# A recurrence followed by an FFN on one core: six more steps whose instructions keep the source's order

## The chip, the cores and the metric

The kernel runs on one core of a Trainium2 chip. The metric is the device time of one execution in microseconds; three executions of the kernel before gave 325.9, 326.82 and 327.14, the median is 326.82. The core has four engines that compute, each with its own queue of instructions, which it works off strictly in order: TensorE (PE; weight loads are listed apart as PEld), VectorE (DVE), ScalarE (ACT) and GpSimd (POOL). SyncE (SP) issues the transfers.

## What is computed

A chunked linear recurrence over 4 x 8 heads of 768 tokens (head size 32, state size 16), and then a feed-forward layer with softplus over all 3072 tokens (256 to 2048 to 256). Cut to what matters:

```python
for c in range(nc):                          # chunks of 32 tokens
    cum = np.cumsum(log_a[chunk])
    M = (C @ B.T) * causal * exp(cum_i - cum_j)
    y = M @ x + (C @ state) * exp(cum)
    state = exp(sum(log_a)) * state + (B * exp(cum_last - cum)).T @ x
h = y_of_all_heads @ w_in                    # 3072 x 256 @ 256 x 2048
g = softplus(h)
out = g @ w_out                              # 3072 x 2048 @ 2048 x 256
```

## The kernel before

**Tiles and units.** The recurrence is worked in 24 units of 128 tokens (unit i = 6 b + u for batch b). The FFN is worked in six tiles of 512 tokens, j = 0 to 5; tile j needs units 4 j to 4 j + 3. For each tile there are 16 slices k of 128 hidden columns.

**The FFN's steps.** A step s stands for one (j, k). Its order over s is: tile 0, k 0 to 7; tile 1, k 0 to 7; tile 0, k 8 to 15; tile 1, k 8 to 15; and from s = 32 on tile 2 and so on, 16 steps each. In step s TensorE does the second product `acc` (six matmuls, in the two `acc` banks) for step s - 4 and the first product `hp` (six matmuls) for step s. The tiles between the two products are `e` (ACT, softplus of hp, L720), `gh` (ACT, its high part, L726) and `gl` (DVE, its low part, L732). Where a tile begins in the `acc` banks (s = 36 for tile 2) `hp` goes ahead of `acc`. When tile 1 is done, in step 35, `finish_part` (L800) adds the half that was kept before: two DVE instructions `o<-acc,half` (L803), one for each `acc` bank, followed by their stores. There is one buffer for each `acc` bank, so the next tile's first product into a bank waits for its `o`.

**The recurrence's work beside it.** From unit 12 on it is spread over the steps, with s0 = 30 + 4 (i - 12):
- step s0 - 4 (28 for unit 12): `split_whole(i)`. ACT then DVE make `c_all` (for even units in `kc`; for odd ones in the tag `c_all` with one buffer) and `b_rows` (two buffers) from the loaded `bc` (ACT L290, DVE L292); between them SP stores `c_all` into `c_rows`, which exists once.
- step s0: `attend_scores(i)`. POOL makes `rm` (L402, two buffers); TensorE `sp` twice, each followed on DVE by `m<-sp,rm` (L457); then DVE `bp` (L417, not for the last unit of a batch) and `cc` (L433, not for the first).
- step s0 + 1: `prefetch(i + 3)`: SP loads `un`, then `bc`, and for even units `gg`.
- for odd i, steps s0 + 2 and s0 + 3: `pair_values` and `pair_ends` of units i - 1 and i (TensorE `zp`, `yp`; DVE `state`, `tb`, `y`, `xl`; ACT `xh`).

So step 31 loads unit 15; step 34 holds `attend_scores(13)` and then `split_whole(14)`; step 35 the two `o` of tile 1 and the loads of unit 16; step 36 `pair_values(12)`; step 37 `pair_ends(12)`; step 38 `attend_scores(14)` and then `split_whole(15)`.

**What sets the order.** The framework has a planner that puts each engine's instructions in an order of its own, by when it reckons their inputs to be there. TensorE's instructions and SP's transfers are always kept in the source's order. For DVE, ACT and POOL, `InOrder` (L118 to L131) does so only while `in_order[0]` is true: each such instruction is pinned behind the instruction that the source issued before it on its engine. An instruction that isn't pinned may be put ahead of pinned ones. Everything up to step 30 is pinned: first what the list `ORDER` gives, which covers the first 28 steps' `hp` and 24 steps' `acc`, then a loop that starts at `AHEAD` = 28 and ends the pinning at `PINNED`:

```python
    for s in range(AHEAD, len(steps) + LAG):
        if s == PINNED:
            in_order[0] = False
        if begins(*steps[s - LAG]):
            begin(s)
        values(s)
        begin(s)
        for f, args in fills[s]:
            f(*args)
```

`in_order[0]` has a second use, in `load_unit` (L252): while it is true and i is 12 or more, a one-element DVE memset of the new `bc` tile stands ahead of its load.

```python
            if in_order[0] and i >= FIRST:
                V.memset(both[:1, :1, :1], 0)
```

All pinned instructions of DVE, ACT and POOL, and all of TensorE's, show the line of the wrapper, L129, in the profile; all transfers show L139.

Of the kernel before, what the change touches and what calls it, by code (L numbers as in the profile page):

```python
# [75 lines left out]
"""  # L76
HALF = NFT // 2
AHEAD = 28
PINNED = 31
LAG = 4  # L80
WRAW = 4
EARLY = 8
# [24 lines left out]
def recurrence_then_ffn(ctx: ExitStack, tc: tile.TileContext, fst, un, alr, w_in, w_out, const, outT):  # L107
# [826 lines left out]
# [3 lines that stand above are left out]
# [63 lines left out]
```

## Time and profile before

| what | us |
|---|---|
| time, median of 3 (lowest to highest) | 326.82 (325.9 to 327.14) |
| the profiled execution's own time | 326.83 |
| its span | 325.1 |
| TensorE busy | 318.3 |
| DVE busy | 190.6 |
| ACT busy | 191.1 |
| POOL busy | 39.4 |

Times in the profile are microseconds from the start of the span. In a timeline row stand the start, the length, the engine (SPq is SyncE's queue), the line, the operation, the tile written and those read, the shape, the number of instructions, and in square brackets the engine's idle time before it with what ended it. In a row of the waits: who waited for whom, us in total, how often, and the longest. A row of stretches has its bounds, its length, the busy time of PE, PEld, DVE, ACT and POOL with the instructions in brackets, the granted TensorE clock, the share of the DMA engines and GB/s. On TensorE a matmul is followed by the next one after some 0.23 us, though its own row is longer, because they are pipelined.

### The profile page before, as it was taken

The page shows a single profiled execution, that of the slowest core. Times are in us where ns is not written, and L with a number is a line of the kernel's source. Part 1 is how long each engine was busy: PE and PEld are TensorE (multiplying, and loading weights), DVE is VectorE, ACT ScalarE, POOL GpSimd, SP SyncE. Part 2 cuts the span into 40 slices and gives each one's busy share as a digit, 9 for nine tenths or more (in the row PEclk, how much of TensorE's full clock was granted, in tenths as well). Part 3 has the DMA queues.
Part 4 walks back from the last instruction along what each step waited for, and adds up shares of the span by engine and source line. Part 5 has one row for each costly group of instructions (what it writes and reads, how often), then busy time and mean ns, then how long its engine had stood idle before and what let it go on. Part 6 is the DMA issues. An engine that isn't in the chain of part 4 may idle for free.

```text
span 325.1 us, 5266 instructions
## 1 busy us (share of the span) xinstructions
PE 318.3 (98%) x1974; PEld 255.7 (79%) x1974; DVE 190.6 (59%) x338; ACT 191.1 (59%) x349; POOL 39.4 (12%) x42
## 2 busy tenths in 40 slices
PE   8999999999999999899999999999999999999996
PEld 3568888888878888588888888888888888888885
DVE  3799767889584566775646746675744433322222
ACT  4898989797877565544433824644633344544450
POOL 3545300210300001102202101012100000000000
PEclk9999999999999999999999999999999999999999
DMA  6949658661732154335125246125201000100001
GB/s 222 394 152 359 212 187 214 176 194 46 246 100 66 65 151 124 107 124 143 32 99 159 70 130 146 51 97 161 86 14 34 0 2 0 53 12 2 1 0 65
DMA packets 25178, 36.53 MB, mean 112 GB/s; under 512 B 2112, under 2 KB 13504, under 8 KB 25152
## 3 DMA queue, kind: packets, MB, share of 16 engines
q1 hardware_dynamic: 25152, 36.19, 36.0%
q8 instruction: 15, 0.25, 0.3%
q14 instruction: 11, 0.09, 0.1%
HBM read 28.74 MB, written 3.24 MB: 98 GB/s over the span
## 4 chain that ended last, share of the span: by engine, by line
PE 88%; DVE 4%; DMA 3%; SPq 2%; issue 2%; ACT 0%; POOL 0%; DVEq 0%; ACTq 0%; POOLq 0%
PE hp L129 38%; PE acc L129 37%; PE yp L129 6%; PE sp L129 4%; PE warm L129 2%; DMA un<-in_un 2%; SPq L139 2%; DMA bc<-in_un 1%; PE zp L129 1%; PE end L129 1%; DVE m L129 1%; DVE w L129 1%; PE gp L129 0%; DVE b_rows L292 0%; DVE o L803 0%
## 5 line engine op out<-in xcount | busy, mean ns | idle before, releaser
L732 DVE TENSOR_TENSOR gl<-e,gh 128x512 fp32r<-128x512 f32 x65 | 49.8, 771 | 50.0 <-ACT gh L726 48.9
L129 PE MATMUL hp<-xh,wih 128*128 128x512 f32 (+1 forms) x204 | 77.6, 380 | 0.0
L129 PE MATMUL hp<-xl,wih 128*128 128x512 f32 (+1 forms) x204 | 76.9, 377 | 0.0
L129 PE MATMUL hp<-xh,wil 128*128 128x512 f32 (+1 forms) x204 | 76.8, 377 | 0.0
L720 ACT ACTIVATE e<-hp 128x512 f32<-128x512 f32 x65 | 38.7, 595 | 64.6 <-PE hp L129 64.2
L129 PE MATMUL acc<-gh,woh 128*128 128x512 f32 x188 | 74.9, 399 | 1.5 <-DVE o L803 1.5
L129 PE MATMUL acc<-gh,wol 128*128 128x512 f32 x188 | 73.4, 390 | 0.1
L129 PE MATMUL acc<-gl,woh 128*128 128x512 f32 x188 | 73.5, 391 | 0.0
L129 PEld LDWEIGHTS hp<-xh,wih 128*128 128x128 f32 x204 | 38.4, 188 | 8.3 <-DVE xl L129 1.0
L726 ACT CAST gh<-e 128x512 fp32r<-128x512 f32 x65 | 40.2, 619 | 6.7 <-PE acc L129 4.0
L129 PEld LDWEIGHTS hp<-xh,wil 128*128 128x128 f32 x204 | 38.3, 188 | 7.1
L129 PEld LDWEIGHTS hp<-xl,wih 128*128 128x128 f32 x204 | 38.4, 188 | 6.9
L129 PEld LDWEIGHTS acc<-gh,woh 128*128 128x128 f32 x188 | 35.4, 188 | 9.0 <-DVE o L803 1.4
L129 PEld LDWEIGHTS acc<-gh,wol 128*128 128x128 f32 x188 | 35.3, 188 | 8.1 <-DVE wol L129 0.6
L129 PEld LDWEIGHTS acc<-gl,woh 128*128 128x128 f32 x188 | 35.4, 188 | 6.4 <-DVE gl L732 0.2
L402 POOL TENSOR_SCALAR_AFFINE_SELECT rm<-fc 128x1024 f32<-128x1024 f32 x11 | 16.8, 1531 | 129.8 <-DVE m L457 97.2
L129 DVE TENSOR_TENSOR gl<-e,gh 128x512 fp32r<-128x512 f32 x31 | 21.5, 701 | 9.6 <-ACT gh L129 9.5
L129 POOL TENSOR_SCALAR_AFFINE_SELECT rm<-fc 128x1024 f32<-128x1024 f32 x13 | 19.0, 1466 | 63.5 <-DVE m L129 58.4
L129 ACT ACTIVATE signs<-wraw 128x512 f16<-128x512 f32 (+1 forms) x32 | 24.1, 776 | 0.0
L129 ACT ACTIVATE e<-hp 128x512 f32<-128x512 f32 x31 | 18.2, 594 | 7.5 <-PE hp L129 7.2
L129 ACT CAST gh<-e 128x512 fp32r<-128x512 f32 x31 | 19.0, 617 | 3.5 <-PE acc L129 3.3
L129 DVE TENSOR_TENSOR m<-sp,rm 128x512 f32<-128x512 f32 x26 | 17.2, 681 | 1.0 <-PE sp L129 1.0
(103 smaller groups left out, 306.8 us busy)
## 6 DMA issues: line engine op xcount, KB each, us to landing
bc<-in_un SPq DMA_DIRECT2D x16, 512.0 KB
wraw<-in_w_in SPq DMA_DIRECT2D x8, 512.0 KB
wraw<-in_w_out SPq DMA_DIRECT2D x8, 512.0 KB
un<-in_un SPq DMA_DIRECT2D x16, 256.0 KB
out_t<-o SPq DMA_DIRECT2D x9, 256.0 KB
gg<-gd SPq DMA_DIRECT2D x16, 128.0 KB
c_rows<-c_all SPq DMA_DIRECT2D x16, 128.0 KB
c_rows<-kc SPq DMA_DIRECT2D x16, 128.0 KB
```

Of the source, the lines that this page charges most:

```text
L129: return lambda *a, **k: tc.keep_in_program_order(f(*a, **k))
L139: tc.keep_in_program_order(nc.sync.dma_start(out, in_))
L402: Pl.affine_select(out=rm.rearrange("p h c i -> p (h c) i"), in_=fc[:, u].rearrange("p h c -> p (h c)").unsqueeze(2).broadcast_to([P, NH * ...
L720: A.activation(e, h, AF.Softplus)
L726: A.copy(gh, e)
L732: V.tensor_tensor(gl, e, gh.bitcast(F32), op=ALU.subtract)
```

## The change

`PINNED` goes from 31 to 37, nothing else:

```diff
-PINNED = 31
+PINNED = 37
```

With it `in_order[0]` stays true for steps 31 to 36. On ACT and DVE the `e`, `gh` and `gl` of these steps, `attend_scores(13)`, `split_whole(14)`, the two `o` of tile 1 and the DVE part of `pair_values(12)` are now pinned in this order. The loads of units 15 and 16 (steps 31 and 35) each get the memset ahead of their `bc`. What comes from step 37 on is free as before.

## The prediction

> **What bounds the kernel now.** I read the page first, then the table of stretches, the waits of TensorE, and the order of instructions of each engine around the places where TensorE stands still. Unit 13, step 34 and so on are counted off in source order, because the profile leaves buffer numbers out. L129 marks an instruction issued while the order is kept; the same instruction issued later shows its own line (L290, L433, L720).
>
> ```profile
> span 325.1 us, 5266 instructions
> PE 318.3 (98%) x1974; PEld 255.7 (79%) x1974; DVE 190.6 (59%) x338; ACT 191.1 (59%) x349; POOL 39.4 (12%) x42
> 88.00:92.50 4.50, 4.27 (x57) 3.09 (x57) 3.51 (x8) 3.04 (x6) 1.06 (x1) 1.00 0.35 81
> 92.50:134.30 41.80, 41.80 (x188) 34.27 (x186) 25.34 (x44) 26.68 (x47) 1.41 (x1) 1.00 0.33 99
> 134.30:138.00 3.70, 2.23 (x27) 1.25 (x30) 3.67 (x5) 1.28 (x4) 1.28 (x1) 1.00 0.29 108
> 138.00:285.00 147.00, 147.00 (x919) 121.67 (x908) 80.23 (x132) 70.74 (x120) 12.87 (x8) 1.00 0.28 79
> PE acc L129 <- DVE o L803: 1.5, 2, 0.9
> ```
>
> In a row of stretches the first number after the bounds is the length, the next the busy time of PE. TensorE is busy 318.3 of 325.1 us, and between 92.5 and 285 us it stands still in one stretch only, 134.3 to 138.0, for 3.70 - 2.23 = 1.47 us. Its order is the source's in both kernels, its granted clock is 1.00 in these rows. So the change can gain only what lies in this gap and in the 0.23 us of the first stretch, and it loses whatever new idle time it puts on TensorE. This is the gap, and the orders of DVE, ACT and POOL that make it:
>
> ```profile
> 134.97 0.47 PE L129 MATMUL acc<-gh,woh 128*128 128x512 f32 x1 [0.55 <-DVE o L803]
> ...
> 136.82 0.50 PE L129 MATMUL acc<-gh,woh 128*128 128x512 f32 x1 [0.92 <-DVE o L803]
> ...
> 137.72 0.43 PE L129 MATMUL zp<-un,bp 128*32 128x64 f32 x16
> ```
>
> ```profile
> 132.28 0.75 DVE L292 SCALAR_TENSOR_TENSOR c_all<-bc,kb,c_all 128x512 fp32r<-128x512 f32 x1 [1.86 <-ACT c_all L290]
> 132.94 1.28 DVE L457 TENSOR_TENSOR m<-sp,rm 128x512 f32<-128x512 f32 x2
> 134.14 0.68 DVE L803 TENSOR_TENSOR o<-acc,half 128x512 f32<-128x512 f32 x1
> 134.74 1.43 DVE L292 SCALAR_TENSOR_TENSOR b_rows<-bc,kb,b_rows 128x512 fp32r<-128x512 f32 x1
> 136.09 0.68 DVE L803 TENSOR_TENSOR o<-acc,half 128x512 f32<-128x512 f32 x1
> 136.69 1.28 DVE L732 TENSOR_TENSOR gl<-e,gh 128x512 fp32r<-128x512 f32 x2
> ```
>
> ```profile
> 127.15 0.60 ACT L720 ACTIVATE e<-hp 128x512 f32<-128x512 f32 x1 [1.47 <-PE hp L129]
> 127.78 0.62 ACT L726 CAST gh<-e 128x512 fp32r<-128x512 f32 x1
> 131.52 0.72 ACT L290 ACTIVATE c_all<-bc,kb 128x512 fp32r<-128x512 f32 x1 [3.11 <-DMA bc<-in_un]
> 132.15 0.58 ACT L720 ACTIVATE e<-hp 128x512 f32<-128x512 f32 x1
> 132.63 0.71 ACT L290 ACTIVATE b_rows<-bc,kb 128x512 fp32r<-128x512 f32 x1
> 133.24 0.61 ACT L726 CAST gh<-e 128x512 fp32r<-128x512 f32 x1
> ```
>
> ```profile
> 134.36 1.28 POOL L402 TENSOR_SCALAR_AFFINE_SELECT rm<-fc 128x1024 f32<-128x1024 f32 x1 [11.29 <-DVE m L457]
> ```
>
> The second product of tile 2 begins in banks that the two o instructions of tile 1 (step 35) must first read. The first o ends at 134.82, the second at 136.77, and TensorE follows at 134.97 and 136.82. They are late because c_all of unit 15, which the source has in step 38, was put ahead of e of step 34 on ACT and ahead of m of unit 13 on DVE, and its data came 3.11 us after ACT had reached it. On the other hand the planner had put gl of step 34 (136.69), bp, cc and both splits of unit 14 out of the way of o.
>
> **The change part by part.** Steps 31 to 36 keep the source's order on DVE, ACT and POOL. Instructions of step 37 and later stay free. I take it, from the code and from the tiles standing in source order in every group that I looked at, that the buffers of one tag are given out in source order. Then bp and cc of units 14 and 15 and b_rows of unit 15 can't pass unit 13's and 14's. But c_all of unit 15 has a tag of its own that only odd units use, so it can still go ahead.
>
> *Removed: cc of unit 13 from 88.71.* It waited for its unit's load with everything behind it:
>
> ```profile
> 88.71 0.48 DVE L433 TENSOR_TENSOR cc<-un,fr 128x128 f32<-128x128 f32 x1 [1.10 <-DMA un<-in_un]
> 89.11 0.68 DVE L129 SCALAR_TENSOR_TENSOR w<-w,signs 128x512 int32<-128x512 int32 x1
> ...
> 89.73 0.06 DVE L129 MEMSET bc<- 1x1 int32 x1
> ```
>
> ```profile
> 89.91 0.40 PE L129 MATMUL acc<-gl,woh 128*128 128x512 f32 x1
> 90.46 0.50 PE L129 MATMUL acc<-gh,wol 128*128 128x512 f32 x1
> ```
>
> ```profile
> 91.25 0.39 PE L129 MATMUL acc<-gh,wol 128*128 128x512 f32 x1
> 91.71 0.71 PE L129 MATMUL yp<-cc,tb 128*128 128x128 f32 x4
> ```
>
> ```profile
> 87.78 1.28 POOL L402 TENSOR_SCALAR_AFFINE_SELECT rm<-fc 128x1024 f32<-128x1024 f32 x1
> ```
>
> At the pitch of 0.23 us between products, 90.46 - 89.91 - 0.23 = 0.32 is lost at the first pair and 91.71 - 91.25 - 0.23 = 0.23 at the second, 0.55 in all. But the next instruction on DVE, w, would now stand beside rm of unit 13, which runs to 87.78 + 1.28 = 89.06, as POOL's order doesn't change. Such pairs block each other: b_rows at 134.74, beside rm at 134.36, takes 1.43 instead of 0.75 and ends at 136.17, 0.53 after rm's end at 135.64. So w ends at about 89.06 + 0.53 = 89.59 instead of 89.79: a gain of **0.2 us**, bounds 0 and 0.55 (no blocking).
>
> *Added: two one-element memsets* (units 15 and 16), each ahead of its bc load, behind gl of steps 31 and 35. A memset of this kind takes 0.06 us (the row at 89.73). Unit 15's buffer was last read by unit 12's split, long done, so the memset waits for nothing, and SP reaches that bc load only at 127.22, after the two c_rows stores and un below, while gl of step 31 is done by about 125. Cost 0; bounds 0 and 0.06 each on DVE.
>
> *Moved on DVE ahead of m of unit 13 and of o:* gl of step 34, then behind m: bp and cc of unit 13, kc and b_rows of unit 14, then the two o. I work it out by assuming that c_all of unit 15 keeps its place ahead of e on ACT, because what makes it free there does not change much: TensorE's order, bc's place in SP's queue. When does its data come?
>
> ```profile
> 123.12 0.74 DVE L129 SCALAR_TENSOR_TENSOR c_all<-bc,kb,c_all 128x512 fp32r<-128x512 f32 x1
> ```
>
> ```profile
> 121.65 1.41 POOL L402 TENSOR_SCALAR_AFFINE_SELECT rm<-fc 128x1024 f32<-128x1024 f32 x1 [32.59 <-DVE m L129]
> ```
>
> ```profile
> 123.92 2.62 SPq L139 DMA_DIRECT2D c_rows<-c_all  x2
> ...
> 127.22 0.45 SPq L139 DMA_DIRECT2D bc<-in_un  x1
> 130.34 1.29 SPq L139 DMA_DIRECT2D c_rows<-kc  x2
> ```
>
> The bc load stands behind the c_rows stores, and those behind c_all of unit 13, which ends at 123.86. Without the two bp ahead of it c_all of unit 13 would start near 121.65, but beside rm, so it ends at 121.65 + 1.41 + 0.53 = 123.6: 0.25 earlier, and ACT's c_all starts at 131.27. (The two stores take 2.62 us here and 1.29 at 130.34; if this falls away too, it is 1.3 us earlier yet. I keep that for the range.) From 131.27, with the pitches of the rows above:
> - ACT: c_all 131.27, e + 0.63 = 131.90, gh + 0.63 = 132.53, done 133.15.
> - DVE: gl of step 34 at 133.18, m at + 0.61 = 133.79, both done at + 1.28 = 135.07.
> - POOL's rm of unit 15 starts 0.14 after m (134.22 to 134.36), so 135.21; bp gets in before it, cc waits: rm from about 135.25 to 136.55.
> - kc at 136.60 (c_all at 123.12 stood 0.06 behind the end of rm), b_rows + 0.66 = 137.26, o + 0.66 = 137.92, second o + 0.60 = 138.52.
> - TensorE: first product at o + 0.83 = 138.75 (134.14 to 134.97), second + 0.77 = 139.52, zp + 0.75 = 140.27, against 137.72.
>
> That is **+2.55 us** in the place of the 1.47 us wait, so that the gap there becomes about 4 us. Bounds of this term: +1.2 (the stores at 1.29) and +2.8 (bc not earlier at all). [...]
>
> *Moved elsewhere:* bp and cc of unit 14 and cc of unit 15 leave their early places; they come after step 36, where DVE has 147.00 - 80.23 = 66.8 us free. c_rows of unit 14 are stored near 137.3 instead of 130.34 and are read by TensorE in step 38, past 144, so that is hidden too; if that cover went, TensorE would wait for the store's landing there. gh of step 36 waits for the product's end as before, and state and tb behind it are due only at yp of step 37, some 3 us later.
>
> Sum: 2.55 - 0.2 = +2.35 on the profiled execution's 326.83 us (span 325.1 and 1.73 around it; the median is 326.82, the same): **329.2 us**.
>
> **The rivals.**
> 1. *c_all of unit 15 doesn't go ahead of gh any more* (its memset, or the shorter queue in front, puts its load past gh in the planner's reckoning). Then e starts when its hp ends, a step's 12 products of 0.227 behind the e at 127.15: 129.87, gh 130.50, gl 131.15, m 131.76 to 133.04, rm to 134.50, kc 134.55, o 135.87, TensorE 136.70, zp 138.22: +0.5 - 0.2, **327.1 us**. Without the blocking by rm o starts 1.15 earlier and zp comes at 137.1: 326.0. For it: ACT's place for c_all lies within one wait for hp (128.4 to 129.85). Against: nothing ahead of its load grows by more than 0.06 us. This ends on the other side, not slower; the point from which it decides is whether bc counts as landed before hp of step 34.
> 2. *c_all goes between e and gh:* gh starts 0.63 earlier than in the forecast, **328.6 us**.
> 3. *DVE's row goes on and rm waits for it* (cc, kc and b_rows follow bp without a break, rm runs beside o): o starts near 136.8, 1.15 less than the forecast, **328.0 us**. For it: DVE has an instruction ready at every end. Against: at 121.65 rm went ahead of the bp that was next on DVE.
> 4. *The change does nothing here:* the planner's order of DVE comes out with the same wait at o: **326.8 us**. Against: gl, bp, cc, kc and b_rows stand ahead of o in the source, and the chain is kept.
>
> **How the numbers follow.** Forecast 0.55, rival 1 0.22, rival 2 0.08, rival 3 0.10, rival 4 0.05. The forecast's own bounds are 1.2 - 0.2 and 2.8, so 327.8 to 329.6. Within 0.5% means 325.2 to 328.5, about what a measurement of this kernel can tell from no change. Of the forecast some 0.45 lies above that and 0.10 within (short stores); rival 2 is half and half; rivals 1, 3 and 4 lie within, but for 0.04 that I keep for gains that no row shows, on top of rival 1 unblocked and the whole 0.55 (325.7). Slower 0.50, same 0.46, faster 0.04. The range runs from rival 1 (327.1, less some of its unblocked form) to the forecast's upper bound with 0.2 us for an unseen stall: 326.5 to 329.8.
>
> **What would show it.** Right: no DVE row of cc near 88.7 waiting for un; on ACT c_all waiting about 3 us for bc near 128 to 131, ahead of e; on DVE gl, m twice, bp, cc, kc, b_rows, o, o in one row between 133 and 139; a wait of acc for o of 3 to 4.5 us and nowhere else one over 0.3. Wrong: e of step 34 right behind hp (rival 1), rm behind b_rows (rival 3), a new wait of TensorE at sp of step 38 for c_rows or at hp of step 37 (bp and cc made late matter after all), or o ahead of kc.

## The result and the profile after

| | median, us | lowest to highest | ratio to the kernel before |
|---|---|---|---|
| before | 326.40 (4 runs) | 325.9 to 327.14 | 1 |
| changed | 330.76 (4 runs) | 329.77 to 332.17 | 1.0135, interval 1.009 to 1.018 |

The change makes the kernel slower by 4.4 us. The forecast had 329.2 us, slower by 2.35, in a range that ended at 329.8: the sign was right, the size was half of it. The profiled execution of the changed kernel took 329.77 us, the fastest of its four.

The head of the changed kernel's page:

```profile
span 328.0 us, 5267 instructions
PE 318.7 (97%) x1974; PEld 256.7 (78%) x1974; DVE 191.4 (58%) x340; ACT 190.9 (58%) x349; POOL 39.9 (12%) x42
```

Its waits of TensorE (us in total, times, longest):

```profile
PE acc L129 <- DVE o L129: 4.2, 1, 4.2
```

Its stretches (bounds, length, busy time of PE, PEld, DVE, ACT and POOL, granted clock, DMA share, GB/s):

```profile
84.00:92.50 8.50, 8.44 (x75) 6.46 (x74) 7.92 (x15) 6.84 (x13) 2.95 (x2) 1.00 0.64 209
134.30:145.00 10.70, 7.50 (x69) 5.81 (x70) 7.37 (x17) 1.23 (x3) 0.60 (x1) 0.84 0.46 147
145.00:285.00 140.00, 140.00 (x849) 115.86 (x848) 76.45 (x124) 68.02 (x116) 12.86 (x8) 1.00 0.27 72
```

One wait of TensorE stands where two stood before: 4.2 us for the first o, in the place of 1.5 for both. From 145 to 285 us TensorE is busy without a break, as before. But the granted clock of the stretch from 134.30 to 145 is 0.84, where the kernel before had 1.00 in all its rows from 88 to 285 us. The same stretch of the changed kernel, cut at 138.06, where the products' rows grow longer, and at 141.48, with as much ahead of it and behind it:

```profile
134.65:138.06 3.41, 0.56 (x3) 0.50 (x4) 3.41 (x8) 0.26 (x1) 0.25 (x1) 1.00 0.16 36
138.06:141.48 3.42, 3.42 (x45) 2.48 (x47) 2.27 (x6) 0.62 (x1) 0.00 (x0) 0.50 0.61 194
141.48:144.90 3.42, 3.42 (x30) 2.72 (x23) 1.34 (x5) 0.00 (x0) 0.00 (x0) 1.00 0.67 230
```

TensorE's timeline there:

```profile
132.90 0.39 PE L129 MATMUL hp<-xh,wil 128*128 128x512 f32 x1
137.50 0.47 PE L129 MATMUL acc<-gh,woh 128*128 128x512 f32 x1 [4.21 <-DVE o L129]
...
138.43 0.63 PE L129 MATMUL acc<-gh,woh 128*128 128x512 f32 x1
138.86 0.63 PE L129 MATMUL acc<-gl,woh 128*128 128x512 f32 x1
139.28 0.63 PE L129 MATMUL acc<-gh,wol 128*128 128x512 f32 x1
139.85 0.65 PE L129 MATMUL zp<-un,bp 128*32 128x64 f32 x16
140.28 1.64 PE L129 MATMUL yp<-m,un 128*32 128x128 f32 x32
141.84 0.50 PE L129 MATMUL acc<-gh,woh 128*128 128x512 f32 x1
142.18 0.39 PE L129 MATMUL acc<-gl,woh 128*128 128x512 f32 x1
```

What to see here: from 138.06 to 141.48 the clock is half. The products stand 0.43 us apart instead of 0.23, and yp takes 1.64 instead of 1.06. From 142.18 on a product's row is 0.39 long again instead of 0.63. So the wait is followed by a second loss that is no wait and shows in no list of waits.

Why o is late is to be read from the timelines of the changed kernel, first ACT's:

```profile
126.03 0.60 ACT L129 ACTIVATE e<-hp 128x512 f32<-128x512 f32 x1 [1.47 <-PE hp L129]
129.05 0.72 ACT L290 ACTIVATE c_all<-bc,kb 128x512 fp32r<-128x512 f32 x1 [2.42 <-DMA bc<-in_un]
129.68 0.60 ACT L129 CAST gh<-e 128x512 fp32r<-128x512 f32 x1
130.19 0.59 ACT L129 ACTIVATE e<-hp 128x512 f32<-128x512 f32 x1
130.81 0.62 ACT L129 CAST gh<-e 128x512 fp32r<-128x512 f32 x1
```

Then DVE's:

```profile
131.47 0.69 DVE L129 TENSOR_TENSOR gl<-e,gh 128x512 fp32r<-128x512 f32 x1 [0.31 <-ACT gh L129]
132.08 1.28 DVE L129 TENSOR_TENSOR m<-sp,rm 128x512 f32<-128x512 f32 x2
133.28 0.28 DVE L129 TENSOR_TENSOR bp<-un,ft 128x128 f32<-128x128 f32 x1
133.47 0.28 DVE L129 TENSOR_TENSOR cc<-un,fr 128x128 f32<-128x128 f32 x1
133.68 1.35 DVE L417 TENSOR_TENSOR bp<-un,ft 128x128 f32<-128x128 f32 x1
134.95 0.48 DVE L433 TENSOR_TENSOR cc<-un,fr 128x128 f32<-128x128 f32 x2
135.36 0.74 DVE L129 SCALAR_TENSOR_TENSOR kc<-bc,kb,kc 128x512 fp32r<-128x512 f32 x1
136.02 0.74 DVE L129 SCALAR_TENSOR_TENSOR b_rows<-bc,kb,b_rows 128x512 fp32r<-128x512 f32 x1
136.68 1.27 DVE L129 TENSOR_TENSOR o<-acc,half 128x512 f32<-128x512 f32 x2
```

And POOL's:

```profile
133.49 1.41 POOL L402 TENSOR_SCALAR_AFFINE_SELECT rm<-fc 128x1024 f32<-128x1024 f32 x1 [11.67 <-DVE m L129]
```

This is the row that the forecast laid out: gl of step 34, m twice, bp, cc, then rm on POOL with DVE held up beside it (1.35 for a bp of 0.28), kc, b_rows, o. Two details differ: c_all of unit 15 (L290) stands one place earlier on ACT, ahead of gh of step 33; and three free instructions (L417, L433 twice) got in ahead of kc.

### The profile page after: what moved, and what is told of

The parts are those of the page before. It is cut to its first block, busy times and chain, and to the rows that moved or that the text cites. A ratio compares the mean times of both kernels' runs of the same rounds, so it can differ in the third digit from the quotient of the medians.

```text
span 328.0 us, 5267 instructions
## 1 busy us (share of the span) xinstructions
PE 318.7 (97%) x1974; PEld 256.7 (78%) x1974; DVE 191.4 (58%) x340; ACT 190.9 (58%) x349; POOL 39.9 (12%) x42
## 4 chain that ended last, share of the span: by engine, by line
PE 87%; DVE 6%; issue 2%; ACT 2%; DMA 1%; SPq 1%; POOL 0%; DVEq 0%; ACTq 0%; POOLq 0%
PE hp L129 37%; PE acc L129 36%; PE yp L129 6%; PE sp L129 3%; DVE m L129 2%; PE warm L129 2%; DMA bc<-in_un 1%; PE zp L129 1%; PE end L129 1%; SPq L139 1%; ACT e L129 1%; DVE w L129 1%; ACT gh L129 1%; DVE c_all L129 1%; PE gp L129 0%
## 5 line engine op out<-in xcount | busy, mean ns | idle before, releaser
L129 DVE TENSOR_TENSOR m<-sp,rm 128x512 f32<-128x512 f32 x28 | 18.5, 681 | 0.9 <-PE sp L129 0.9
```

What stands on the lines that cost most here:

```text
L129: return lambda *a, **k: tc.keep_in_program_order(f(*a, **k))
```

## The experiments

Each ran beside the kernel before on the same chip. In the diffs "-" is the changed kernel unless another is named. The experiments with extra products add work on TensorE whose result nobody reads; none leaves anything out.

**1. Work for TensorE during the wait.** It keeps the wait and takes away TensorE's idleness.

```diff
+        if s == 36:
+            spare = ps.tile([P, 512], F32, tag="ps", name="spare")
+            for _ in range(3):
+                products(2, 4, spare, 0, 512)
         values(s)
```

> The changed kernel with 18 extra first products (some 18 x 0.227 = 4.1 us) into a bank that nobody reads, put on TensorE ahead of the second product of step 36, where it waits for o. Theory (the wait of 4.3 us also halves the granted clock afterwards, which in the profiled run cost another 1.45 us): the clock stays at 1.00 in this stretch, o starts where it did, and the time falls by 1.4 to 2.9 us, from 330.76 to 327.9 to 329.4 us, with less spread from run to run. Rival (only the wait for o costs; the slow matmuls behind it cost nothing that is not the wait): 330.8 us.

Measured: 329.46 us (328.92 to 331.82, 5 runs), ratio 1.0092 (1.0053 to 1.0132). That is 1.3 less than the changed kernel had in the runs of the result, just short of what was expected, and with a spread that didn't shrink (one run of 331.82 at 0.997), so both were run again side by side.

> The changed kernel unchanged, timed again on the chip that times the next two, so that the granted clock of every run can be set beside its time. [...]

> The changed kernel with the 18 extra first products during the wait, as in the first experiment, on the same chip as the last one. Theory: clock 0.999 to 1.000 in every run, o where it was, 1.4 to 2 us less than the last one. Rival: no more than 0.5 us less.

Measured on one chip: the changed kernel 331.30 us (330.40 to 333.31, 6 runs), the granted clock 0.995 in three runs (330.40, 331.21, 331.22) and 0.990 in the other three (331.37, 332.32, 333.31); with the extra products 328.90 us (328.31 to 330.07, 6 runs), clock 0.998 to 1.000. The kernel before had 326.49 there (17 runs). The extra products take 2.4 us off, more than expected. In the trace o sets the same start, and the same stretch has its clock back. TensorE's timeline with the extra products (the run beside the changed kernel):

```profile
137.09 0.39 PE L129 MATMUL spare<-xh,wil 128*128 128x512 f32 x1
137.48 0.50 PE L129 MATMUL acc<-gh,woh 128*128 128x512 f32 x1
137.81 0.40 PE L129 MATMUL acc<-gl,woh 128*128 128x512 f32 x1
...
140.30 0.50 PE L129 MATMUL acc<-gh,woh 128*128 128x512 f32 x1
```

Its `o` on DVE:

```profile
136.74 1.28 DVE L129 TENSOR_TENSOR o<-acc,half 128x512 f32<-128x512 f32 x2
```

Its stretch:

```profile
134.30:145.00 10.70, 10.70 (x92) 8.34 (x91) 8.51 (x20) 2.85 (x6) 0.66 (x1) 1.00 0.45 149
```

o starts at 136.74 and the second product at 137.48, against 136.68 and 137.50 in the first profile of the changed kernel, so the late o is untouched. From there to the next step's product it takes 140.30 - 137.48 = 2.82 us instead of 141.84 - 137.50 = 4.34: in these two executions the halved clock costs 1.5 us. Between the medians on that chip it is 2.4 of the 4.8 us that the changed kernel loses. The other 2.4 are the longer wait, less the gain at cc.

**2. The split of unit 15 pinned.**

```diff
-        plan(max(s - 4, AHEAD), split_whole, i)
+        plan(max(s - 4, AHEAD), kept(split_whole) if i == 15 else split_whole, i)
```

`kept` sets `in_order[0]` to true while the function runs.

> The changed kernel with the split of unit 15 (step 38) pinned too, so that its c_all can't stand ahead of gh of step 33 on ACT. Theory (gl of step 34, m and then o are late because ACT waits for that c_all's data): o starts some 1.4 us earlier, TensorE's wait falls from 4.3 to 2.9 us; with the clock still halved 329.3 us, with the clock at 1.00 326.5 to 327.9 us. Rival (the row bp, cc, kc, b_rows ahead of o sets the time alone): same as the changed kernel, 330.8 us.

Measured: 328.59 us (327.74 to 330.67, 9 runs), ratio 1.0075 (1.0049 to 1.01). Its wait of TensorE, in the profiled run at 0.995:

```profile
PE acc L129 <- DVE o L129: 2.8, 1, 2.8
```

The 3.41 us at half clock there, and as much ahead of them:

```profile
133.79:137.20 3.41, 0.63 (x4) 0.55 (x4) 3.41 (x8) 0.60 (x1) 0.20 (x1) 1.00 0.17 38
137.20:140.61 3.41, 3.41 (x45) 2.47 (x47) 1.60 (x6) 0.62 (x1) 0.00 (x0) 0.50 0.59 193
```

The wait is 2.8 us, as worked out, so the wait of ACT for that c_all's data is worth 1.4 of it. The clock now halves in some runs only: the four runs at 1.000 took 327.74 to 328.58, the five at 0.995 or 0.990 took 328.59 to 330.67. To see whether that is the clock or something else in those runs:

> The changed kernel with the split of unit 15 pinned and 12 extra first products (2.7 us) in the wait of 2.8 us that is left. Theory: the clock, which fell in some runs of that kernel without them, stays at 1.00 in all; the time is that of its runs without the fall, 327.7 to 328.2 us, against a median of 328.6. Rival: the same 328.6 us.

Measured: 327.46 us (326.72 to 327.88, 12 runs), clock 1.00 in all. The spread is 1.2 us instead of 2.9, and no run shows the fall, so the fall of the clock and the time that goes with it are gone. But nine of the 12 runs lie below the fastest of the four without the fall (their median is 328.4), on another chip; what takes off the further 0.9 us is open. And the clock is not all of the spread: the first four runs of the changed kernel, all at 0.995, spread over 2.4 us.

**3. The split of unit 14 behind o.**

```diff
-        plan(max(s - 4, AHEAD), split_whole, i)
+        plan(35 if i == 14 else max(s - 4, AHEAD), split_whole, i)
```

> The changed kernel with the split of unit 14 moved from step 34 to behind the two o of step 35. Theory (kc and b_rows of 0.66 us each delay o, as does what the planner fits in front of them): o starts 1.3 to 2.9 us earlier (the larger figure if bp and cc of the next units move behind o as well), TensorE's wait falls to 1.5 to 3.0 us: 326.4 to 329.4 us, by the clock. Rival (only c_all of unit 15 counts): 330.8 us.

Measured: 333.29 us, ratio 1.0193 (1.015 to 1.0237): a miss. The part at o came out, and more (the wait is 1.1 us, expected 1.5 to 3.0), but another wait took its place. The waits of TensorE:

```profile
PE sp L129 <- DMA c_rows<-kc: 4.5, 1, 4.5
PE acc L129 <- DVE o L129: 1.1, 1, 1.1
```

SP's timeline:

```profile
137.91 0.37 SPq L139 DMA_DIRECT2D bc<-in_un  x1
142.34 1.18 SPq L139 DMA_DIRECT2D gg<-gd  x2
143.57 1.31 SPq L139 DMA_DIRECT2D c_rows<-kc  x2
```

Stretches of 3.41 us there, and what comes behind:

```profile
144.59:148.00 3.41, 0.00 (x0) 0.00 (x0) 0.69 (x1) 0.98 (x2) 0.00 (x0) 1.00 0.52 130
148.00:151.41 3.41, 2.61 (x8) 2.35 (x9) 1.74 (x3) 1.44 (x2) 0.32 (x1) 0.50 0.05 11
151.41:154.83 3.42, 3.42 (x9) 2.64 (x8) 1.88 (x2) 0.00 (x0) 1.35 (x1) 0.50 0.96 243
```

In step 35 the moved split came behind that step's loads, so its c_rows stores stood behind gg on SP, which was issued at 142.34, and sp of step 38 had to wait for them. I had moved a step past SP's queue without counting it. The rows also show what this wait of 4.5 us did: 3.41 us with TensorE idle, then 6.83 us at half clock (148.00 to 154.83). In the first 3.41 of these it is busy for 2.61 us only, and the clock stays at 0.50 for 3.42 more.

**4. Both of these edits.**

> Both of the last two edits on the changed kernel. Theory: o starts behind m, bp and cc of unit 13 alone, TensorE waits some 1.1 us, the clock stays at 1.00, and the time is that of the kernel before less the gain at the early cc (0.4 us) and some 0.3 us: 325.4 to 326.2 us. Rival (pinning these six steps costs elsewhere too): over 327.5 us.

Measured: 331.87 us, ratio 1.0161 (1.0123 to 1.02). The wait for o is gone, and the same wait at sp (4.6 us) takes its place, with a mean clock of 0.989 in the profiled run (0.990 in experiment 3's). It says nothing on the six steps until the side effect is mended.

**5. The moved split ahead of step 35's loads,** without and with the split of unit 15 pinned:

```diff
-        plan(max(s - 4, AHEAD), split_whole, i)
+        if i != 14:
+            plan(max(s - 4, AHEAD), split_whole, i)
         plan(s, attend_scores, i)
+        if i == 13:
+            plan(s + 1, split_whole, 14)
         plan(s + 1, prefetch, i + 3)
```

> The changed kernel with the split of unit 14 moved behind the two o of step 35, this time ahead of that step's loads, so that its c_rows stores don't stand behind gg of unit 16 on SP. Theory (the 4.5 us at sp of step 38 in the first form came from that queue alone): no wait at sp, TensorE waits 1.1 us for o, clock at 1.00: the kernel before less 0.4 to 0.8 us, 325.6 to 326.1 us. Rival (c_rows come too late in any form): over 328 us.

Measured: 326.39 us (325.35 to 326.98, 10 runs), ratio 0.9994 (0.9979 to 1.0009): no wait at sp, 0.9 us for o, clock 1.00. The time is 0.3 us above what was expected, but this one edit takes back the whole loss.

> The last one with the split of unit 15 pinned too. Theory: no wait for o and none at sp: the kernel before less some 1.9 us at o and 0.35 us at cc, 324.2 us; the six steps kept in order are then no worse than the two pins alone (324.6 us). Rival (keeping six steps in order costs in some other place): 326 us or more.

Measured: 324.28 us (323.98 to 325.16, 7 runs), ratio 0.9939 (0.9917 to 0.9961). With these two splits put right, keeping six more steps in order costs nothing that shows; the rival falls. In its trace TensorE never stands still here, with gl, m, bp, cc and o in one row on DVE:

```profile
130.75 0.69 DVE L129 TENSOR_TENSOR gl<-e,gh 128x512 fp32r<-128x512 f32 x1 [2.03 <-ACT gh L129]
131.36 1.28 DVE L129 TENSOR_TENSOR m<-sp,rm 128x512 f32<-128x512 f32 x2
132.56 0.28 DVE L129 TENSOR_TENSOR bp<-un,ft 128x128 f32<-128x128 f32 x1
132.76 0.28 DVE L129 TENSOR_TENSOR cc<-un,fr 128x128 f32<-128x128 f32 x1
132.96 1.28 DVE L129 TENSOR_TENSOR o<-acc,half 128x512 f32<-128x512 f32 x2
```

Its stretch:

```profile
130.00:145.00 15.00, 15.00 (x113) 12.16 (x112) 12.51 (x29) 8.91 (x16) 1.56 (x2) 1.00 0.38 119
```

**6. Single pins on the kernel before** (order kept to step 30): the split of unit 15 alone, and with cc of unit 13.

```diff
-        plan(max(s - 4, AHEAD), split_whole, i)
+        plan(max(s - 4, AHEAD), kept(split_whole) if i == 15 else split_whole, i)
```

```diff
-        scale_c(i)
+        (kept(scale_c) if i == 13 else scale_c)(i)
```

> The kernel before (order kept to step 30) with the split of unit 15 alone pinned, so that m of unit 13 and o need not wait for its data. Theory: o follows the last product of tile 1 at once, the 1.47 us that TensorE waits in the kernel before shrinks to 0 to 0.3, the clock stays at 1.00: some 1.4 us less than the kernel before, 325.0 us. Rival (o then waits for something else in the same place): within 0.4 us of the kernel before.

Measured: 325.12 us (324.56 to 325.82, 12 runs), ratio 0.9964 (0.9951 to 0.9977).

> As the last one, with cc of unit 13 pinned behind bp too, so that it no longer waits for its load at 88.7. Theory: a further 0.35 us, which the changed kernel gained there: 324.6 us. Rival (rm takes the gain back): as the last one, 325.0 us.

Measured: 324.56 us (324.15 to 325.06, 6 runs), ratio 0.9949 (0.9931 to 0.9967). Both came out within 0.15 us. So two places of the kernel before, c_all of unit 15 ahead of m and cc of unit 13 at 88.7, are worth 1.8 us together (326.35 to 324.56), and both can be had without the row that the change puts ahead of o. This version and the one with 324.28 are the fastest of the study; their intervals overlap.

## Why the prediction was half right

**The wait for o: right.** The chain ran through gl, m, bp, cc, rm, kc, b_rows and o as forecast. The changed kernel's profile runs ahead of the other by 0.73 us at 84 us, before anything that the change moves (the same DVE instruction at 83.59 instead of 84.32), and by 1.11 from 91 us on. With that added, o starts at 136.68 + 1.11 = 137.79, forecast 137.92, and the second product at 137.50 + 1.11 = 138.61, forecast 138.75. That it fits so closely is partly luck, for two errors cancel. c_all's data came 1.1 us early, since the c_rows stores ahead of bc took 1.37 us instead of 2.62, the short case of the forecast's range. Of the seven other pairs of c_all's stores in the kernel before six took 1.31 to 1.37 us and one 2.00; the forecast had built on an odd one. But c_all also went ahead of one more gh, which took 0.5 of this, so that gl, m and bp ran 0.6 us ahead of the chain. And the two free cc that got in ahead of kc, behind the bp that rm held up, took another 0.4; the forecast had put that bp and these cc (units 14 and 15) behind step 36. Experiment 1 gives the wait, less the gain at cc, as 2.4 us in its second set, against 2.35 forecast, and as 3.0 in its first.

**The clock: the step that failed.** The forecast's last line of the chain, "TensorE: first product at o + 0.83 [...] second + 0.77, zp + 0.75 = 140.27", took the products behind the wait at the full-speed pitch and so put the clock's cost at nothing. In its own first part it had read "its granted clock is 1.00 in these rows" from a kernel whose waits there are 0.55 and 0.92 us, and it made a gap of about 4 us out of them without asking what the clock does in such a gap. The second of two products, zp and yp ran at half clock in its place, and the next step's product came at 141.84 + 1.11 = 142.95 instead of 138.95, 4.0 us late instead of 2.55. Between two executions, with and without the extra products, this term is 1.5 us; between the medians of experiment 1's second set it is 2.4 us, and half of the changed kernel's runs there have a mean clock of 0.990 instead of 0.995, which is, as an estimate, twice the time at half clock. The profiles show how long the clock stays at 0.50 behind the wait, 3.42 us in the changed kernel and 3.41 in experiment 2, and that TensorE was not idle throughout in the 3.41 us ahead of it: it was busy for 0.56 us of them in the changed kernel, and for 0.63 in experiment 2. What sets the moment of the fall and its length they do not show.

**The range** ended at 329.8 because every bound in it was a bound on the wait. With the 3.42 us at half clock of the changed kernel's profile on top, or with twice as long, as in experiment 3 (1.5 us or, as an estimate, twice that), it would have reached 331.3 or 332.8.

**The gain at cc: under-sized, 1.11 - 0.73 = 0.38 instead of 0.2.** The forecast let rm hold w back. In fact w, at 86.85, got in ahead of the second rm, at 87.04, which was itself held up, and the next instruction paid. DVE's timeline of the changed kernel:

```profile
86.85 0.77 DVE L129 SCALAR_TENSOR_TENSOR w<-w,signs 128x512 int32<-128x512 int32 x1
87.55 1.74 DVE L129 TENSOR_TENSOR wol<-w,woh 128x512 fp32r<-128x512 f32 x1
```

POOL's:

```profile
85.81 2.95 POOL L129 TENSOR_SCALAR_AFFINE_SELECT rm<-fc 128x1024 f32<-128x1024 f32 x2 [18.71 <-DVE m L129]
```

The two rm take 2.95 us instead of 2.52 (1.28 and 1.72), wol beside the second takes 1.74 instead of 0.68, and TensorE's idle time in the first stretch falls from 0.23 to 8.50 - 8.44 = 0.06 us. The forecast's upper bound of 0.55 was too wide: the 0.32 at the first pair of products goes, and 0.07 right behind it, but the 0.23 ahead of yp stays (90.15 to 90.60 in the changed kernel, 0.45 for a pitch of 0.23), where yp begins 0.06 us behind the end of tb on DVE (90.54). Not every DVE instruction beside an rm took longer: in the kernel before the first o, at 134.14, took the same 0.68 beside the rm of 134.36 as the second took behind it.

**The rest.** The memsets took 0.06 us each and held nothing up, as forecast. The late c_rows cost nothing, and bp and cc of units 14 and 15 nothing but the 0.4 us ahead of o (TensorE is busy without a break from 145 to 285). Rival 1 fell: c_all of unit 15 did go ahead, and even one place further, ahead of gh of step 33. As the reason given against this rival had it, the memset did not put its load back. Experiment 2 shows what rival 1 would have been worth: 1.4 us of wait. Rival 2 fell with it (c_all did not stand between e and gh of step 34), and so did rival 4 (the wait is 4.2 us, not 1.5). Rival 3 fell at this place: rm went first, and bp beside it took 1.35 us. How much of the loss rm makes here by itself was not tried.

## What to carry to other kernels

Where a change makes TensorE wait as long as here, 2.8 us or more, in one piece, add the clock: look in the table of stretches whether the granted clock falls behind it, and put 3.4 us at half speed (as in the changed kernel's profile) or 6.8 (as in experiment 3's) into the upper bound. Keeping the source's order helps only as far as the source's order is good: ask of each pinned row which instruction in it another engine waits for, and put that one first, here o ahead of the next unit's split. A pin on the one instruction that gets ahead of its data does the same without the row.

## What the runs showed of the hardware

Behind the long waits of TensorE the granted clock stood at 0.50: for 3.42 us behind the 4.2 us of the changed kernel, for 3.41 behind the 2.8 of experiment 2, and for 6.83 behind the 4.5 of experiment 3. By the mean clock of each run it fell in all ten runs of the changed kernel, whose wait is 4.2 us in the profile of the result, and in five of nine with 2.8 us; behind the waits of 0.55 to 1.1 us for o (the kernel before, experiments 3 and 5) the rows show 1.00. One of the 17 runs of the kernel before beside experiment 1's second set shows 0.995 all the same (328.51 us), and nothing on record says where it fell. In the 3.41 us ahead of the fall TensorE was busy for 0.56 us in the changed kernel, for 0.63 in experiment 2 and not at all in experiment 3. There the clock stayed at 0.50 behind a first 3.41 us in which TensorE was busy for 2.61. What a wait between 1.1 and 2.8 us does to the clock no run shows. Why half of the changed kernel's second set of runs had about twice the time at half clock (an estimate: 0.010 of 330 us is 3.3 us, at half clock 6.6 us) stays open too, because those runs have no trace. 12 or 18 matmuls whose result is thrown away during the wait keep the clock of each run at 0.997 to 1.00, and pay for themselves (331.30 to 328.90 us with 18) though they are pure extra work.
